# Scores of a Nyström attention: which matmul operand is read or written with a step

## The chip, the cores and the metric

The kernel runs on one core of one Trainium2 chip. Its metric is the time of one execution on the device, in microseconds.

## The reference, cut to what matters

Batch 4, 8 heads, 576 positions, 64 values per head; 32 landmarks, each the mean over 18 neighbouring positions. Three softmax matrices, a Newton iteration for a pseudo-inverse, and then two FFN layers (512 to 2048 to 512) over the 2304 tokens, one with mish, one with silu.

```python
q_lm = q.reshape(B, H, m, S // m, D).mean(axis=3)
k_lm = k.reshape(B, H, m, S // m, D).mean(axis=3)
...
A = sm(q, k_lm)
Bm = sm(q_lm, k_lm)
C = sm(q_lm, k)
Z = Bm.transpose(0, 1, 3, 2) / (...)
for _ in range(6):
    Z = 2 * Z - Z @ Bm @ Z
return (A @ Z @ C @ v).astype(np.float32)
...
x = _moe_ref(x=x, **moe_kwargs)
return _moe2_ref(x=x, **moe2_kwargs)
```

All of it is float32. The FFN's matmuls split each operand into a high and a low fp32r part and add three products (`PASSES`, L20).

## The kernel before, in words

**Attention.** The 32 pairs of batch and head are worked in eight groups of four heads (class `Group`, L1109). For a group, `load` (L1118) brings the keys `kn` and the queries `qn` as 128 partitions (4 heads x 32 landmarks) by 18 positions by 64 values, and `load_v` (L1135) the values. `transposed` (L1165) turns them into `Tk` and `Tq`, nine TensorE transposes each: the tile has 128 partitions (64 values of an even and of an odd position) and [9 position pairs, 4 heads, 32 landmarks] along a partition, so that neighbours along a partition are neighbouring landmarks, and two position pairs of one head lie 128 float32 apart. (Group 1 keeps its `Tk` and `Tq` in two borrowed tiles, which the trace calls `wp`.) `main` (L1203) makes the landmark means `lmT`, the small matrix Bm and the Newton steps.

`scores` (L1189) makes the scores of landmarks against positions: for four heads and two parities it issues eight matmuls of 64 x 32 weights out of `lmT` with 288 moving columns, on eight different 64*32 tiles of the array, into two PSUM banks (four heads in four times 32 partitions of each). TensorE runs each float32 matmul as two instructions, so a call is 16 of them in the trace. It is called twice for a group, by `c_side` (L1373) with the keys and by `a_side` (L1440) with the queries; the argument `mov` gives the moving operand of a head and parity. What comes next on the 288 columns: for C, VectorE's row maxima (`nm2`, L1385), ScalarE's exponentials `e_c` (L1395), and TensorE's transposes of 96 columns at a time; for A, VectorE's 32 x 32 transposes of the scores into `at` (L1453) and the softmax there.

The order of the columns in PSUM matters to these followers. The 288 columns of C are ordered as (w, l, c) and those of A as (l, j), in the letters of these two lines, in which c, w and j count position pairs and l landmarks:

```python
1, lambda e, h: kT[64 * e:64 * e + 64, :, h, :].rearrange("p (c w) l -> p w l c", c=VC)
s_, s_a = self.scores(0, lambda e, h: qT[64 * e:64 * e + 64, :, h, :].rearrange("p j l -> p l j"))
```

**FFN.** The first layer's units are matmuls on 128 x 128 tiles in fp32r (`emit_h`, L973, into `h`; `emit_o`, L1002, into `y`). They begin while the attention of later groups is still under way, and fill TensorE between its pieces. `projection` (L680) multiplies the first layer's weights `wa` by the attention's small matrices `ut`: 16 float32 TensorE instructions on the same eight 64*32 tiles, with 512 or 256 moving columns that are neighbours. Transposes of the identity (`y<-ident`, `h<-ident`, L1593) fill TensorE where nothing else is due.

**What sets the order.** All engines' programs are laid out when the kernel is built, by a planner (class `Line`, L70) with a cost for each instruction (`cost`, L101) and due times for chains of steps. The cost of a matmul goes by its number of columns and the size of its tile, not by steps in its operands. SyncE issues the loads in program order: group 2's `vn` takes the buffer of group 0's (two buffers, L1098 and L1136), and so waits for group 0's last C matmuls (`t<-vn,ect`, L1417); weights (`aw`, `wst`) are queued behind it.

Of the kernel before, what the change touches and what calls it, by code (L numbers as in the profile page):

```python
# [61 lines left out]
def f32(ap):  # L62
    return ap.bitcast(FP32)
# [347 lines left out]
def kernel(  # L411
# [15 lines left out]
    LM = 32  # L427
    J = S // LM
    J2 = J // 2
    SH = S // 2  # L430
# [4 lines left out]
    VC = 96 // LM  # L435
# [25 lines left out]
    def slots(n, of, **kw):  # L461
# [30 lines left out]
        out=twice.rearrange("p (a d) -> p a d", a=2),  # L492
# [18 lines left out]
    def until(cond):  # L511
        while not cond():
            yield "W"

    def marked(*m):
        return lambda: all(a in marks for a in m)
# [148 lines left out]
    def at_of(b):  # L665
        if b not in a_t:
            a_t[b] = at_p.tile([128, 2, GB, 2, SH], F32R, tag=f"at{b}", name=f"at{b}")
        return a_t[b]
# [434 lines left out]
    def bc(ap, n):  # L1103
        return ap.rearrange("p (j o) -> p j o", o=1).to_broadcast([128, ap.shape[1], n])
# [4 lines left out]
    class Group:  # L1109
# [76 lines left out]
            yield "W"  # L1186
            marks.add((g, "T" + nm))

        def scores(self, i, mov):  # L1189
            s = [self.pairs.take([128, 512], FP32) for e in range(2)]  # L1190
            for r in range(2):
                for h in range(HG):
                    e = (h + r) % 2
                    T.matmul(
                        out=s[e][0][32 * h:32 * h + 32, 0:SH],
                        lhsT=self.lmT[64 * e:64 * e + 64, i, 32 * h:32 * h + 32],
                        rhs=mov(e, h),
                        start=True,
                        stop=True,
                    )  # L1200
            return s, [x[0][:, 0:SH] for x in s]
# [171 lines left out]
        def c_side(self):  # L1373
            g = self.g
            yield from until(marked((g, "lmT"), (g, "Tk")))
            yield from until(lambda: self.pairs.open(2))
            kT = self.tT["k"]
            s_, s_c = self.scores(
                1, lambda e, h: kT[64 * e:64 * e + 64, :, h, :].rearrange("p (c w) l -> p w l c", c=VC)
            )  # L1380
            marks.add((g, "sc"))
            yield "V+"
            nm2 = s_p.tile([128, 2], FP32, tag="nm2", name="nm2")
            for e in range(2):
                V.tensor_reduce(out=nm2[:, e:e + 1], in_=s_c[e], axis=AX.X, op=ALU.max)  # L1385
            yield "V"
            nmc = s_p.tile([128, 1], FP32, tag="nmc", name="nmc")
            V.tensor_reduce(out=nmc, in_=nm2, axis=AX.X, op=ALU.max, negate=True)
            yield "A+"
            e_c = a_p.tile([128, 2, SH], FP32, tag="ec", name="ec", bufs=2)  # L1390
            scr = s_p.tile([128, 1], FP32, tag="scr", name="scr")
            scm = s_p.tile([128, 1], FP32, tag="scm", name="scm")
            sc2 = s_p.tile([128, 2], FP32, tag="sc2", name="sc2")
            for e in range(2):
                A.activation(out=e_c[:, e], in_=s_c[e], func=ACTF.Exp, bias=nmc, accum_out=sc2[:, e:e + 1])  # L1395
                Ring.give(s_[e])
            line.add(self.total(scm, sc2, scr), self.kind("N"), "V", line.end + 0.17)
            yield "T+"
            yield from until(lambda: g == 0 or (g - 1, "cv") in marks)
            ect = a_p.tile([96, VI, 128], FP32, tag="ect", name="ect")  # L1400
            for i0 in (0, 3):
                yield from until(self.banks.open)
                pe = self.banks.take([96, 3, 128], FP32)
                for i in range(i0, i0 + 3):
                    T.transpose(
                        out=pe[0][:, i - i0, :], in_=e_c[:, i % 2, 96 * (i // 2):96 * (i // 2) + 96], identity=ident
                    )
                yield "W"
                VA.copy(out=ect[:, i0:i0 + 3, :], in_=pe[0])
                Ring.give(pe)  # L1410
                yield "T+"
            yield from until(self.banks.open)
            pu_ = self.banks.take([128, D], FP32)
            pu = pu_[0]
            for i in range(VI):
                for h in range(HG):
                    T.matmul(  # L1417
                        out=pu[32 * h:32 * h + 32],
                        lhsT=ect[:, i, 32 * h:32 * h + 32],
                        rhs=self.vn[:, h, i, :],  # L1420
                        start=(i == 0),
                        stop=(i == VI - 1),
                    )
            marks.add((g, "cv"))
            yield "V"
            yield from until(lambda: (g, "y") in marks and ("w", scr.name) in line.seen)
            VAs.scaled(out=self.yu[:, LM:], in_=pu, scalar1=scr)
            Ring.give(pu_)
            yield "W"
            marks.add((g, "u"))  # L1430
# [9 lines left out]
        def a_side(self):  # L1440
            g = self.g
            yield from until(marked((g, "lmT"), (g, "Tq"), (g, "sc")))
            yield from until(lambda: self.pairs.open(2))
            qT = self.tT["q"]
            s_, s_a = self.scores(0, lambda e, h: qT[64 * e:64 * e + 64, :, h, :].rearrange("p j l -> p l j"))
            marks.add((g, "scores"))
            if g == 1:
                for t_ in self.borrowed:
                    Ring.give(t_)
            yield "V+"  # L1450
            at = a_p.tile([128, J, LM], FP32, tag="at", name="at", bufs=2)
            for e in range(2):
                V.transpose(out=at[:, e * J2:(e + 1) * J2, :].rearrange("p j l -> p (j l)"), in_=s_a[e])  # L1453
                Ring.give(s_[e])
            am = s_p.tile([128, J], FP32, tag="am", name="am")
            yield "V+"
            V.tensor_reduce(out=am, in_=at, axis=AX.X, op=ALU.max)
            yield "W"
            VP.tensor_tensor(out=at, in0=at, in1=bc(am, LM), op=ALU.subtract)
            yield "A+"  # L1460
            A.activation(out=at, in_=at, func=ACTF.Exp, scale=scale)
            yield "V+"
            asm = s_p.tile([128, J], FP32, tag="asm", name="asm")
            V.tensor_reduce(out=asm, in_=at, axis=AX.X, op=ALU.add)
            yield "V+"
            V.tensor_scalar(out=asm, in0=asm, scalar1=1e-9, scalar2=None, op0=ALU.add)
            ar = s_p.tile([128, J], FP32, tag="ar", name="ar")
            yield "V+"
            V.reciprocal(out=ar, in_=asm)
            yield "W"  # L1470
            VP.tensor_tensor(out=at, in0=at, in1=bc(ar, LM), op=ALU.mult)
            yield from until(lambda: g == 0 or (g - 1, "a_t") in marks)
            yield "V+"
            ar_t = a_p.tile([128, 2, SH], FP32, tag="a_t", name="a_t", bufs=1)
            V.transpose(out=ar_t.rearrange("p e n -> p (e n)"), in_=at.rearrange("p j l -> p (j l)"))
            yield "W"
            at = at_of(self.b)
            VA.copy(out=at[:, 0, self.hg], in_=ar_t)
            yield "W"
            (P if g < LOPOOL else VPx).tensor_tensor(out=at[:, 1, self.hg], in0=ar_t, in1=f32(at[:, 0, self.hg]), op=ALU.subtract)  # L1480
            a_ready[self.b, self.hg] = line.end + 0.12 + SLACK
            yield "W"
            marks.add((g, "a_t"))
# [53 lines left out]
    def o_time(u):  # L1537
        ph, t, f, first, last = u
        if first and not y_r.any_of(KD):
            return LATE  # L1540
        return max(g_ready.get((ph, t, f), LATE), w_ready.get(("o", 0, f), LATE))
# [3 lines left out]
    while todo or flight:  # L1545
# [32 lines left out]
        to = o_time(flight[0]) if flight else LATE  # L1578
# [81 lines left out]
```

## Time and profile before

| | us |
|---|---|
| median of 3 runs (832.25 to 833.1) | 832.32 |
| the profiled execution | 831.79 |
| its span in the trace | 830.0 |
| TensorE busy | 815.3 |
| VectorE busy | 561.9 |
| ScalarE busy | 443.2 |

The time of the profiled execution is 1.79 us longer than the span, in which the trace has its first and last record. A busy TensorE is one with a matmul under way, from its issue to its modelled end; matmuls overlap, so a batch is better measured from its first start to the start of what follows it. In the rows below, `64*32` after a matmul is the tile of the array, `64x288` what it reads, `t`, `y` and `h` are PSUM banks, and an idle time in brackets is that of the engine just before the row. All matmuls carry "f32" there; those of the FFN (`g,wo`, `wo,xg`, `at,wp`) are fp32r, those of the scores and the projections float32.

### The profile page before, as it was taken

How to read it: one execution, taken by the hardware profiler on the slowest of the kernel's cores; microseconds unless marked ns; L12 is line 12 of the kernel's file. 1: busy time of each engine (PE TensorE's matmuls, PEld its weight loads, DVE VectorE, ACT ScalarE, POOL GpSimd, SP SyncE). 2: the span in 40 equal slices, each digit the busy share in tenths (PEclk: the TensorE clock that was granted, in tenths of full speed). 3: DMA queues.
4: the chain of work that ended last, by engine and by line, in shares of the span. 5: the costliest groups of instructions: out<-in, count | busy, mean ns of one | idle time of the engine just before them, and what ended most of it. 6: DMA issues, size and time to landing. Idle time of an engine off the chain costs nothing.

```text
span 830.0 us, 15406 instructions
## 1 busy us (share of the span) xinstructions
PE 815.3 (98%) x5920; PEld 728.1 (88%) x5920; DVE 561.9 (68%) x1274; ACT 443.2 (53%) x981; POOL 124.7 (15%) x168
## 2 busy tenths in 40 slices
PE   9999999999999999999999999999999999999997
PEld 6787788777989999989998988988988988988985
DVE  7978876674667787853639999676655567555542
ACT  5475667757656656442526665436445436544422
POOL 2010321020000001000001122211232211232210
PEclk9999999999999999999999999999999999999999
DMA  8774024210044566541135222103100001100002
GB/s 279 237 212 160 29 87 127 67 39 30 29 143 154 169 199 199 174 147 46 60 101 174 77 102 92 36 1 106 48 1 0 1 1 37 40 0 1 1 1 76
DMA packets 41737, 72.29 MB, mean 87 GB/s; under 512 B 3776, under 2 KB 31936, under 8 KB 41664
## 3 DMA queue, kind: packets, MB, share of 16 engines
q1 hardware_dynamic: 40768, 70.53, 26.7%
q8 instruction: 46, 0.75, 0.4%
q10 hardware_dynamic: 896, 0.79, 0.3%
q14 instruction: 27, 0.22, 0.1%
HBM read 57.15 MB, written 14.16 MB: 86 GB/s over the span
## 4 chain that ended last, share of the span: by engine, by line
PE 93%; DVE 3%; DMA 2%; ACT 1%; issue 1%; ACTq 0%; SPq 0%
PE y L262 50%; PE h L262 34%; PE t L262 9%; DMA kn<-in_k_dram 1%; DMA wst<-in_moe_w_out_dram 1%; DVE m L262 0%; DVE wa L262 0%; DVE z L262 0%; ACT L262 0%; DMA out_dram<-z 0%; DVE lmk L262 0%; ACTq L274 0%; DVE nm L262 0%; DVE at L262 0%; DVE st L262 0%
## 5 line engine op out<-in xcount | busy, mean ns | idle before, releaser
L262 PE MATMUL y<-g,wo 128*128 128x288 f32 x1536 | 228.2, 300 | 0.6 <-DVE g L262 0.6
L262 PEld LDWEIGHTS y<-g,wo 128*128 128x128 f32 x1536 | 208.6, 188 | 16.8 <-issue 15.2
L262 PE MATMUL y<-wo,xg 128*128 128x512 f32 x693 | 180.0, 394 | 0.0
L262 PEld LDWEIGHTS y<-wo,xg 128*128 128x128 f32 x693 | 128.4, 188 | 20.8
L262 DVE TENSOR_TENSOR z<-h,z 128x384 f32<-128x384 f32 x161 | 87.7, 555 | 70.8 <-PE h L262 68.5
L262 PE MATMUL h<-at,wp 128*128 128x288 f32 x768 | 118.0, 300 | 0.7 <-ACT z L262 0.6
L262 PEld LDWEIGHTS h<-at,wp 128*128 128x128 f32 x768 | 105.3, 188 | 8.4 <-issue 6.5
L262 ACT ACTIVATE z<-h 128x288 f32<-128x288 f32 x128 | 51.5, 413 | 72.6 <-PE h L262 71.7
L262 DVE TENSOR_TENSOR g<-z,g 128x288 fp32r<-128x288 f32 x118 | 53.0, 461 | 51.0 <-ACT g L262 42.4
L262 ACT ACTIVATE z<-z 128x384 f32<-128x384 f32 x95 | 49.8, 525 | 34.4 <-DVE z L262 34.1
L262 PE MATMUL h<-xg,wp 128*128 128x384 f32 x288 | 57.8, 335 | 0.0
L262 PE MATMUL h<-xg,wf 128*128 128x384 f32 x282 | 56.6, 335 | 0.0
L262 DVE TENSOR_TENSOR xg<-z,xg 128x384 fp32r<-128x384 f32 x76 | 42.3, 557 | 20.2 <-ACT xg L262 20.1
L262 ACT CAST g<-z 128x288 fp32r<-128x288 f32 x120 | 49.9, 435 | 8.4 <-PE y L262 6.9
L262 PEld LDWEIGHTS h<-xg,wp 128*128 128x128 f32 x288 | 51.3, 188 | 3.2
L262 PEld LDWEIGHTS h<-xg,wf 128*128 128x128 f32 x282 | 50.3, 188 | 3.1
L262 DVE SCALAR_TENSOR_TENSOR m<-wst,m 128x512 int32<-128x512 int32 x64 | 46.4, 728 | 0.7
L262 PE MATMUL y<-wo,wp 128*128 128x512 f32 x171 | 44.9, 394 | 0.0
L262 ACT ACT_TABLE_LOAD x31 | 39.8, 1283 | 9.4 <-DVE nmc L262 3.5
L262 POOL TENSOR_TENSOR g<-z,g 128x288 fp32r<-128x288 f32 x10 | 8.4, 840 | 234.9 <-ACT g L262 156.5
L262 ACT CAST xg<-z 128x384 fp32r<-128x384 f32 x76 | 38.9, 512 | 1.6
L262 PEld LDWEIGHTS y<-wo,wp 128*128 128x128 f32 x171 | 31.7, 188 | 5.3
(245 smaller groups left out, 1164.8 us busy)
## 6 DMA issues: line engine op xcount, KB each, us to landing
wst<-in_moe_w_out_dram SPq DMA_DIRECT2D x32, 512.0 KB, 5.8
wst<-in_moe_w_in_dram SPq DMA_DIRECT2D x22, 512.0 KB, 5.2
kn<-in_k_dram SPq DMA_DIRECT2D x8, 576.0 KB, 6.2
vn<-in_v_dram SPq DMA_DIRECT2D x8, 576.0 KB, 6.6
yh<-ysb SPq DMA_DIRECT2D x32, 144.0 KB, 1.8
ysb<-yh SPq DMA_DIRECT2D x32, 144.0 KB, 3.0
ys<-ysb SPq DMA_DIRECT2D x32, 144.0 KB, 2.2
qn<-in_q_dram SPq DMA_DIRECT2D x7, 576.0 KB, 4.1
```

What stands on the lines that cost most here:

```text
L262: r = getattr(self.nc[e], name)(**kw)
```

## The change

`scores` takes a second function, `to`, which gives the order in which the 288 output columns are written. The moving operand keeps the order in which it lies in `Tk` and `Tq`: runs of 32 neighbouring landmarks, nine runs for a matmul. The output is written with a step instead, 3 columns for the keys and 9 for the queries, so that each score lands in the column where it was before. Number and order of the instructions are the same on each engine, and so are their waits; the forms of the 128 score matmuls differ.

```diff
-        def scores(self, i, mov):
+        def scores(self, i, mov, to):
...
-                        out=s[e][0][32 * h:32 * h + 32, 0:SH],
+                        out=to(s[e][0][32 * h:32 * h + 32, 0:SH]),
...
             s_, s_c = self.scores(
-                1, lambda e, h: kT[64 * e:64 * e + 64, :, h, :].rearrange("p (c w) l -> p w l c", c=VC)
+                1,
+                lambda e, h: kT[64 * e:64 * e + 64, :, h, :].rearrange("p (c w) l -> p c w l", c=VC),
+                lambda s: s.rearrange("p (w l c) -> p c w l", l=LM, c=VC),
             )
...
-            s_, s_a = self.scores(0, lambda e, h: qT[64 * e:64 * e + 64, :, h, :].rearrange("p j l -> p l j"))
+            s_, s_a = self.scores(
+                0, lambda e, h: qT[64 * e:64 * e + 64, :, h, :], lambda s: s.rearrange("p (l j) -> p j l", j=J2)
+            )
```

## Rows read from the trace of the kernel before

**Rows 1.** The page: TensorE's busy time, and the chain that ended last by engine.

```profile
PE 815.3 (98%) x5920; PEld 728.1 (88%) x5920; DVE 561.9 (68%) x1274; ACT 443.2 (53%) x981; POOL 124.7 (15%) x168
...
PE 93%; DVE 3%; DMA 2%; ACT 1%; issue 1%; ACTq 0%; SPq 0%
```

**Rows 2.** TensorE's waits, longest first: total us, times, longest us.

```profile
PE h L262 <- DVE z L262: 1.9, 1, 1.9
```

**Rows 3.** Score matmuls: duration ns min/median/max, first and last start us, forms.

```profile
L262 PE MATMUL t<-Tk,lmT x96: 492/500/511, 54.2 to 199.3; 64*32 64x288 f32 x96
L262 PE MATMUL t<-Tq,lmT x96: 727/766/786, 61.5 to 205.6; 64*32 64x288 f32 x96
```

**Rows 4.** TensorE's timeline, groups 2 and 3: start us, busy us, what.

```profile
54.21 1.05 PE L262 MATMUL t<-Tk,lmT 64*32 64x288 f32 x16
...
80.68 0.88 PE L262 MATMUL t<-Tk,lmT 64*32 64x288 f32 x16
81.49 2.17 PE L262 MATMUL h<-at,wp 128*128 128x288 f32 x14
...
93.39 1.40 PE L262 MATMUL t<-Tq,lmT 64*32 64x288 f32 x16
94.72 0.80 PE L262 MATMUL y<-g,wo 128*128 128x288 f32 x4
```

**Rows 5.** TensorE's timeline, two batches of projections and what follows each.

```profile
44.05 0.66 PE L262 MATMUL t<-wa,ut 64*32 64x256 f32 x16
44.64 1.59 PE L262 MATMUL h<-at,wp 128*128 128x288 f32 x10
...
121.11 1.09 PE L262 MATMUL t<-wa,ut 64*32 64x512 f32 x16
122.13 2.63 PE L262 MATMUL y<-g,wo 128*128 128x288 f32 x18
```

**Rows 6.** TensorE's groups by form: busy us, mean ns of one | idle before.

```profile
L262 PE MATMUL y<-g,wo 128*128 128x288 f32 x1536 | 228.2, 300 | 0.6 <-DVE g L262 0.6
L262 PE MATMUL y<-wo,xg 128*128 128x512 f32 x693 | 180.0, 394 | 0.0
...
L262 PE MATMUL t<-wa,ut 64*32 64x512 f32 x240 | 16.9, 601 | 0.0
...
L262 PE MATMUL t<-wa,ut 64*32 64x256 f32 x32 | 1.7, 388 | 0.1
```

**Rows 7.** VectorE's timeline, 54 to 98 us, where it waits for scores.

```profile
62.97 0.85 DVE L262 STREAM_TRANSPOSE at<-t 128x288 f32<-128x288 f32 x2 [0.95 <-PE t L262]
...
81.67 0.82 DVE L262 TENSOR_REDUCE nm<-t 128x1 f32<-128x288 f32 x2 [1.12 <-PE t L262]
```

**Rows 8.** TensorE's timeline, groups 0 and 1.

```profile
12.23 1.39 PE L262 MATMUL y<-Tq,lmT 64*32 64x288 f32 x16
...
15.41 2.07 PE L262 MATMUL y<-wp,lmT 64*32 64x288 f32 x29
17.41 0.53 PE L262 MATMUL t<-ident,ec 128*96 128x128 f32 x3
...
19.69 0.88 PE L262 MATMUL t<-vn,ect 96*32 96x64 f32 x48
```

**Rows 9.** VectorE's timeline, groups 0 and 1: its waits from 12 to 30 us.

```profile
12.56 0.82 DVE L262 TENSOR_REDUCE nm<-y 128x1 f32<-128x288 f32 x2 [0.53 <-PE y L262]
13.73 0.85 DVE L262 STREAM_TRANSPOSE at<-y 128x288 f32<-128x288 f32 x2 [0.35 <-PE y L262]
...
29.20 0.29 DVE L262 TENSOR_SCALAR wa<-wa 128x256 int32<-128x256 int32 x1 [0.68 <-ACT wa L262]
```

**Rows 10.** SyncE's timeline: the loads of group 2's values and of weights.

```profile
20.63 0.33 SPq L274 DMA_DIRECT2D vn<-in_v_dram  x1
21.01 3.37 SPq L274 DMA_DIRECT2D aw<-in_moe_w_in_dram  x4
```

**Rows 11.** ScalarE's timeline: its wait for the weights.

```profile
28.73 0.43 ACT L262 ACTIVATE wa<-aw 128x256 f32<-128x256 f32 x1 [3.48 <-DMA aw<-in_moe_w_in_dram]
```

## The prediction

> **What bounds the kernel now.** I read the page first. TensorE is busy for 98% of the span, and it makes up 93% of the chain that ended last [rows 1]: an edit on TensorE counts unless something else then holds the chain. The list of TensorE's waits says how often that happens: its longest wait in the whole run is 1.9 us, and it has that once [rows 2]. What lies behind the last scores (205.6 us [rows 3]) is a stream of matmuls whose inputs come out of earlier matmuls, so a microsecond won in the attention should stay won to the end.
>
> Then the instructions that the diff edits. Each group of four heads has two batches of score matmuls, "k" (for C) and "q" (for A), of 16 TensorE instructions each: eight matmuls, two instructions for each, on eight different tiles of the array. The reader is to see that k and q have the same shape, the same weights' shape and the same count, and yet one k instruction lasts 500 ns and one q instruction 766 ns [rows 3]. They differ in the order in which the moving operand is read: k takes 3 elements 1536 bytes apart and then goes one on, q takes 9 that are 512 bytes apart. So the order of reading sets the price. In the timeline a k batch occupies TensorE from its start to the start of the next instruction for 81.49 - 80.68 = 0.81 us, and a q batch for 94.72 - 93.39 = 1.33 us [rows 4]. The batches of the other groups look alike; only group 2's k batch is longer, with 1.05 us of busy time instead of 0.88 [rows 4].
>
> **What the change does to a batch.** It removes no instruction, adds none and moves none; no DMA, wait or queue is passed. In both batches the moving operand is now read in runs of 32 neighbours, and the output is written with a step: 3 columns for k, 9 for q. What VectorE and ScalarE read from PSUM afterwards lies where it lay, so their terms are nothing, without any cover.
>
> *The reading.* The trace has batches of the same kind that read neighbours: the projections, 16 instructions on eight 64*32 tiles. With 256 columns they occupy 44.64 - 44.05 = 0.59 us, with 512 columns 122.13 - 121.11 = 1.02 us [rows 5]. That is (1.02 - 0.59)/256 = 1.68 ns per column and 0.59 - 0.43 = 0.16 us fixed. For 288 columns: 0.16 + 0.48 = 0.64 us. So the k batch would win 0.81 - 0.64 = 0.17 us and the q batch 1.33 - 0.64 = 0.69 us, together 0.86 us per group, if writing costs nothing.
>
> *The writing.* No matmul before writes PSUM with a step, so its price is bounded. The lower end is nothing: the writes can't get cheaper than those of neighbouring columns in rows 5, which excludes a gain. The upper end is the worst price that the trace shows for a stepped access, the q reading: 1.33 us per batch, for both kinds. I take the lower end, for this reason. The fp32r matmuls of the FFN last 300 ns for 288 columns and 394 ns for 512, which is 0.42 ns per column, while the float32 matmuls of the projections last 388 ns for 256 and 601 ns for 512, which is 0.83 ns per column [rows 6]. PSUM thus takes columns twice as fast as one float32 instruction makes them, and the score matmuls are float32. A write that takes twice as long per column would still be covered, if the two steps which a float32 column takes end in one place one after the other. If they are instead two sweeps over all columns, this cover is gone, and that is the first rival.
>
> **Where the savings go.** The batches of groups 2 to 7 run from 54.2 to 205.6 us [rows 3], in the stage in which TensorE's order mixes attention and FFN. There the savings are 6 x 0.86 = 5.2 us. VectorE is the engine that could be late next. But it waits for the scores: 0.95 us ahead of group 2's q transposes, 1.12 us ahead of group 3's k maxima [rows 7]. By the latter point groups 2 and 3 have saved 0.17 + 0.69 + 0.17 = 1.03 us, so VectorE's gap just holds it. I count the 5.2 us in full.
>
> Groups 0 and 1 lie in the first 20 us: the q batch at 12.23 us and both batches of group 1 from 15.41 to 17.41 us [rows 8]. That is 1.7 us of TensorE work. In this stage VectorE and the loads count too. VectorE waits 0.53 us for group 0's k scores and 0.35 us for its q scores, and then has no idle time until 28.5 us [rows 9]. On the other side, group 2's values are loaded into a buffer that group 0's last C matmuls (from 19.69 us) free, and SyncE issues that load at 20.63 us, with the first layer's weights queued behind it at 21.01 us [rows 8, 10]. ScalarE later waits 3.48 us for these weights, and VectorE 0.68 us for ScalarE [rows 9, 11]. So an earlier TensorE also brings the weights earlier. Between 0 and 1.7 us I take 0.8 us, near the middle, because VectorE's own two waits let it start its run at most 0.9 us earlier.
>
> **Sum**: 5.2 + 0.8 = 6.0 us off. The profiled execution took 831.79 us, which gives 825.8 us. The median of the three runs shown, 832.32 us, is 0.5 us above it, so the forecast for a median is **826.3 us**. Its own range is 825.4 us (all 6.9 us are kept) to 828.8 us (the first two groups give nothing, and a third of the rest is taken up by VectorE).
>
> **The rivals.**
>
> *1. PSUM takes stepped columns at half the rate, and float32 doesn't cover it.* Then the 0.48 us of columns in a batch become 0.97 us and a batch 1.13 us. k loses 0.32 us, q wins 0.20 us: 0.12 us lost per group, 1.0 us in all, 833.3 us, which I call no change: 0.2%, or 1.7 us, is about what a measurement of this kernel can tell from nothing. For it: the write of neighbours is known only at two columns per 0.83 ns, and nothing in the trace shows the two steps of a float32 column side by side. Against it: the cover of rows 6.
> This rule stands in the Trainium skill, Advanced Engine Details and Errata, section Memory Cachelines: PSUM is accessed in lines of two float32 values, and any pattern that isn't contiguous slows matmuls considerably. No run here shows it yet; by it the change would come out near this rival's time. The same section asks for at least two hits on a 16-byte line of SBUF. The trace agrees only in part: both k and q leave the line after each element, and q pays far more than k [rows 3].
>
> *2. The stepped write is as dear as the stepped read of q (the other side: slower).* Both batches then take 1.33 us. q wins nothing and k loses 0.52 us, 8 x 0.52 = 4.2 us, 836.5 us. It decides from a price per column that I can give: k and q now take 0.81 + 1.33 = 2.14 us together, so they break even at 1.07 us each, which is (1.07 - 0.16)/288 = 3.2 ns per column, 1.9 times the price of neighbours. From 2.1 times on the loss is over 0.2%; below 1.7 times the gain is over 0.2%. For it: a stepped access on the other side of the same instruction does cost 2.4 times (1.33 - 0.16 = 1.17 us against 0.48 us). Against it: k reads with a step as well, and pays 0.65 us, 1.35 times; so step alone isn't dear.
>
> *3. The savings are taken up.* VectorE or the weights hold the chain in the attention, and only about half is left: 3 us, 829.3 us. For it: VectorE's gaps of about 1 us are hardly larger than what is saved ahead of them [rows 7]. Against it: TensorE hardly waits for VectorE [rows 1, 2].
>
> *4. The change doesn't do what it says*: q's 766 ns come from something other than the order of reading, and both batches stay as they are, 832.3 us. Little speaks for it, since k and q share everything else [rows 3].
>
> **How the numbers follow.** The forecast has 0.52, rival 3 has 0.08: faster 0.60. Rival 1 has 0.15 and rival 4 has 0.03: same 0.18. Rival 2, with prices from 2.1 times upward, has 0.22. The range reaches from 824.8 us, a little below the forecast's own low end, to 834.5 us: it takes in the forecast, rivals 1, 3 and 4, and the mild end of rival 2, and leaves out 836.5 us.
>
> **What the profile after would show.** Right: k and q instructions of equal length, about 388 + 32 x 0.83 = 415 ns; batches of 0.64 us both in groups 3 to 7; VectorE's waits for at and nm shorter; the attention's last group some 6 us earlier, and the rest unchanged. The reading is right but the writing isn't free: equal k and q instructions, longer than 415 ns; at about 415 + 240 = 655 ns rival 1 holds, at 766 ns rival 2. If k and q still differ, the write's price depends on its step, 3 against 9 columns. If the batches shrink as forecast and the time doesn't, rival 3 holds, and TensorE's waits for VectorE or the loads will have grown. The forecast is wrong as soon as one batch takes more than about 0.97 us, the point where the gain falls below 0.2%.

## The result, and the profile after

| | before | after |
|---|---|---|
| median, us | 832.71 (6 runs, 832.25 to 834.81) | 825.88 (6 runs, 825.0 to 828.75) |
| ratio to before | 1 | 0.9917, 95% interval 0.9896 to 0.9938 |
| profiled execution / its span, us | 831.79 / 830.0 | 827.49 / 825.7 |
| TensorE busy, us | 815.3 | 808.5 |

The changed kernel is faster by 6.8 us, 0.8%. The forecast was 826.3 us, which is 6.0 us less than the 832.3 us it started from.

First the score matmuls, in the view of one tile's instructions (duration ns min/median/max, first and last start us, forms), to be held against [rows 3]:

```profile
L262 PE MATMUL t<-Tk,lmT x96: 402/415/427, 54.5 to 195.1; 64*32 64x288 f32 x96
L262 PE MATMUL t<-Tq,lmT x96: 402/415/428, 61.6 to 201.0; 64*32 64x288 f32 x96
```

Both kinds last 415 ns, where they were 500 and 766 ns. The last one starts at 201.0 instead of 205.6 us. The batches in TensorE's timeline, against [rows 4]:

```profile
80.02 0.71 PE L262 MATMUL t<-Tk,lmT 64*32 64x288 f32 x16
80.66 2.36 PE L262 MATMUL h<-at,wp 128*128 128x288 f32 x14
...
92.57 0.72 PE L262 MATMUL t<-Tq,lmT 64*32 64x288 f32 x16
93.22 0.79 PE L262 MATMUL y<-g,wo 128*128 128x288 f32 x4
```

A k batch takes 80.66 - 80.02 = 0.64 us and a q batch 93.22 - 92.57 = 0.65 us. Held against before, group 3's k batch starts 0.66 us earlier than in [rows 4], what follows it 0.83 us, its q batch 0.82 us, and what follows that 1.50 us: the gain comes at the batches. VectorE's waits for scores, against [rows 7]:

```profile
62.39 0.85 DVE L262 STREAM_TRANSPOSE at<-t 128x288 f32<-128x288 f32 x2 [0.36 <-PE t L262]
...
80.84 0.82 DVE L262 TENSOR_REDUCE nm<-t 128x1 f32<-128x288 f32 x2 [0.95 <-PE t L262]
```

VectorE still waits, 0.36 us where it was 0.95, and 0.95 us where it was 1.12.

One part of the profiled execution has nothing to do with the change: the first loads came later. TensorE's timeline of the kernel after has two waits for them which the profiled execution of before hadn't:

```profile
8.20 0.55 PE L262 MATMUL h<-ident,kn 128*128 128x128 f32 x3 [1.41 <-DMA kn<-in_k_dram]
...
10.39 0.52 PE L262 MATMUL h<-ident,wp 128*128 128x128 f32 x3 [0.44 <-DMA wp<-in_q_dram]
...
12.78 0.24 PE L262 MATMUL t<-lmT 64*32 64x32 f32 x5
```

The same row in the kernel before, where group 0's scores could begin:

```profile
11.50 0.24 PE L262 MATMUL t<-lmT 64*32 64x32 f32 x5
```

So this execution began its scores 1.28 us later, and yet ended 4.3 us earlier. It is also the second slowest of the six. The experiments' profiles, with edits that can't touch the loads, have these matmuls anywhere between 11.7 and 12.7 us. Part of the spread of a few microseconds among runs comes in here, and two profiles are only compared from this point on.

### The profile page after: what moved, and what is told of

It reads as the page before. It is cut to its first block, busy times and chain, and to the rows that moved or that the text cites. A ratio compares the mean times of both kernels' runs of the same rounds, so it can differ in the third digit from the quotient of the medians.

```text
span 825.7 us, 15406 instructions
## 1 busy us (share of the span) xinstructions
PE 808.5 (98%) x5920; PEld 727.3 (88%) x5920; DVE 562.3 (68%) x1274; ACT 443.1 (54%) x981; POOL 124.6 (15%) x168
## 4 chain that ended last, share of the span: by engine, by line
PE 92%; DVE 4%; DMA 1%; ACT 1%; issue 1%; ACTq 0%; SPq 0%
PE y L262 50%; PE h L262 34%; PE t L262 8%; DMA wp<-in_q_dram 1%; DVE m L262 1%; DVE wa L262 0%; DVE at L262 0%; DVE z L262 0%; DMA out_dram<-z 0%; DVE lmk L262 0%; ACTq L274 0%; DVE g L262 0%; DVE wp L262 0%; DVE nm L262 0%; ACT wp L262 0%
```

## The experiments

**The theory.** The order in which the moving operand is read sets the length of a score instruction; the stepped write costs a second step per column, which float32 covers; and what TensorE saves goes through to the end. Rivals: something of the queries themselves made them slow; a stepped write costs nothing in any case; part of the saving is taken up by VectorE or the loads.

### One kind of scores alone

Keys only (e1), the queries' line as it was before:

```diff
-                0, lambda e, h: qT[64 * e:64 * e + 64, :, h, :], lambda s: s.rearrange("p (l j) -> p j l", j=J2)
+                0, lambda e, h: qT[64 * e:64 * e + 64, :, h, :].rearrange("p j l -> p l j"), lambda s: s
```

Expected: 

> Only the keys' scores read neighbours and write with a step of 3; the queries' scores are as before. If the two batches add up along TensorE's stream: k instructions 415 ns, q instructions 766 ns, k batches 0.64 us, and 8 x 0.17 = 1.4 us off the time before. If a stage takes part of it up (the rival), under 0.7 us off.

Queries only (e2), the keys' lines as they were before:

```diff
-                lambda e, h: kT[64 * e:64 * e + 64, :, h, :].rearrange("p (c w) l -> p c w l", c=VC),
-                lambda s: s.rearrange("p (w l c) -> p c w l", l=LM, c=VC),
+                lambda e, h: kT[64 * e:64 * e + 64, :, h, :].rearrange("p (c w) l -> p w l c", c=VC),
+                lambda s: s,
```

Expected: 

> Only the queries' scores read neighbours and write with a step of 9; the keys' scores are as before. If the two batches add up: k instructions 500 ns, q instructions 415 ns, and 8 x 0.68 = 5.4 us off the time before, the rest of the change's 6.8 us. If the gains overlap or are taken up, e1 and e2 together differ from the change by more than 1.5 us.

| | median, us | ratio to before (832.75 us) |
|---|---|---|
| e1, keys only | 832.3 | 0.9991 (0.9980 to 1.0002) |
| e2, queries only | 827.89 | 0.9939 (0.9923 to 0.9954) |

The instructions have the expected lengths, here of e1 and then of e2:

```profile
L262 PE MATMUL t<-Tk,lmT x96: 402/415/427, 54.8 to 198.8; 64*32 64x288 f32 x96
L262 PE MATMUL t<-Tq,lmT x96: 692/762/786, 61.9 to 205.0; 64*32 64x288 f32 x96
```

```profile
L262 PE MATMUL t<-Tk,lmT x96: 492/500/508, 53.6 to 195.3; 64*32 64x288 f32 x96
L262 PE MATMUL t<-Tq,lmT x96: 402/415/427, 60.9 to 201.2; 64*32 64x288 f32 x96
```

The queries bring 0.61% or 5.1 us. By its times the keys' share, 0.09%, can't be told from nothing, nor from the expected 1.4 us, since its interval reaches from a gain of 1.7 us to a loss of 0.2 us. Together they make 5.8 us against the change's 6.8 us, less than 1.5 us apart, so the two add up as far as the times can tell. The traces tell more, at the end of the next part.

### Where in the program the savings lie

Both edits under a condition on the group, `g < 2` in e3 and `g > 1` in e4; the other groups are as before:

```diff
...
+                (lambda e, h: qT[64 * e:64 * e + 64, :, h, :]) if g < 2
+                else lambda e, h: qT[64 * e:64 * e + 64, :, h, :].rearrange("p j l -> p l j"),
+                (lambda s: s.rearrange("p (l j) -> p j l", j=J2)) if g < 2 else lambda s: s,
...
```

Expected of e3: 

> The change in groups 0 and 1 alone, the first 20 us. The prediction's sum has 0.8 us off for them. If all of TensorE's work counts there, 1.7 us off; if the loads and VectorE hold this stage, 0 to 0.3 us off.

Expected of e4: 

> The change in groups 2 to 7 alone. The prediction's sum has 5.2 us off for them, counted in full. If VectorE takes part of it up, under 4 us off.

| | median, us | ratio to before (832.75 us) |
|---|---|---|
| e3, groups 0 and 1 | 831.6 | 0.9983 (0.9971 to 0.9994) |
| e4, groups 2 to 7 | 828.39 | 0.9945 (0.9930 to 0.9960) |

Groups 2 to 7 bring 4.6 us by the ratio, with an interval from 3.3 to 5.8 that holds the 5.2 us counted for them, and also the rival's under 4 us. Groups 0 and 1 bring 1.4 us, with an interval from 0.5 to 2.4 that holds both the 0.8 and the 1.7 us and excludes that the loads take it up wholly. The two profiles say more here, because in both of them the first loads came alike: the matmuls in front of group 0's scores start at 12.73 us in each. The timelines of TensorE and of SyncE in e3, where groups 0 and 1 are changed:

```profile
12.73 0.24 PE L262 MATMUL t<-lmT 64*32 64x32 f32 x5
...
19.51 0.88 PE L262 MATMUL t<-vn,ect 96*32 96x64 f32 x48
...
51.38 0.27 PE L262 MATMUL t<-lmT 64*32 64x32 f32 x8
```

```profile
20.45 0.33 SPq L274 DMA_DIRECT2D vn<-in_v_dram  x1
```

And in e4, where they are not:

```profile
12.73 0.25 PE L262 MATMUL t<-lmT 64*32 64x32 f32 x5
...
20.91 0.88 PE L262 MATMUL t<-vn,ect 96*32 96x64 f32 x48
...
52.80 0.27 PE L262 MATMUL t<-lmT 64*32 64x32 f32 x8
```

```profile
21.85 0.33 SPq L274 DMA_DIRECT2D vn<-in_v_dram  x1
```

The C matmuls that free group 0's values start 1.40 us earlier, the load of group 2's values and the weights behind it go out 1.40 us earlier, and 30 us later group 2's landmark matmuls still start 1.42 us earlier. So the loads move with TensorE. ScalarE's wait for these weights ends 1.67 us earlier, first e3 and then e4:

```profile
28.42 0.45 ACT L262 ACTIVATE wa<-aw 128x256 f32<-128x256 f32 x1 [2.81 <-DMA aw<-in_moe_w_in_dram]
```

```profile
30.09 0.43 ACT L262 ACTIVATE wa<-aw 128x256 f32<-128x256 f32 x1 [3.63 <-DMA aw<-in_moe_w_in_dram]
```

The same can be done for the whole attention: a profile's stretch from group 0's landmark matmuls (12.73 us above, 11.50 us before, 12.78 us after) to group 2's, and from these to what follows the last q batch. It leaves out the first loads and all that comes after the attention. What follows the last q batch starts at 206.12 us in e3 and at 202.50 us in e4. The marks before, after, in e1 and in e2 (in these two group 0's matmuls start at 12.59 and 12.06 us):

```profile
51.46 0.27 PE L262 MATMUL t<-lmT 64*32 64x32 f32 x8
...
206.26 1.06 PE L262 MATMUL h<-at,wp 128*128 128x288 f32 x6
```

```profile
51.70 0.27 PE L262 MATMUL t<-lmT 64*32 64x32 f32 x8
...
201.34 1.06 PE L262 MATMUL h<-at,wp 128*128 128x288 f32 x6
```

```profile
52.01 0.27 PE L262 MATMUL t<-lmT 64*32 64x32 f32 x8
...
205.67 1.06 PE L262 MATMUL h<-at,wp 128*128 128x288 f32 x6
```

```profile
50.82 0.27 PE L262 MATMUL t<-lmT 64*32 64x32 f32 x8
...
201.54 1.06 PE L262 MATMUL h<-at,wp 128*128 128x288 f32 x6
```

| | groups 0 and 1, us | groups 2 to 7, us |
|---|---|---|
| before | 39.96 | 154.80 |
| e3, groups 0 and 1 changed | 38.65 | 154.74 |
| e4, groups 2 to 7 changed | 40.07 | 149.70 |
| after | 38.92 | 149.64 |
| e1, keys only | 39.42 | 153.66 |
| e2, queries only | 38.76 | 150.72 |

The stretch of groups 2 to 7 repeats to 0.06 us where the scores are alike. There the change saves 5.16 us (before to after) and 5.04 us (e3 to e4), so the 5.2 us counted are kept in full. The keys alone save 1.14 us and the queries alone 4.08 us, together 5.22 us: the keys' share is real, and the two add up. The stretch of groups 0 and 1 repeats less well: the change saves 1.04 us there from before to after, and 1.42 us from e4 to e3, where TensorE has 1.7 us less work.

### What the stepped write costs

e5 takes the step out of the write:

```diff
-                lambda s: s.rearrange("p (w l c) -> p c w l", l=LM, c=VC),
+                lambda s: s.rearrange("p (j l) -> p j l", l=LM),
...
-                0, lambda e, h: qT[64 * e:64 * e + 64, :, h, :], lambda s: s.rearrange("p (l j) -> p j l", j=J2)
+                0, lambda e, h: qT[64 * e:64 * e + 64, :, h, :], lambda s: s.rearrange("p (j l) -> p j l", l=LM)
```

Expected: 

> The scores read neighbours and also write neighbours, so the score columns lie in another order and what follows takes them as they lie: the softmaxes mix up positions, at the same sizes and durations. If the step in the write is free: instructions of 415 ns and batches of 0.64 us, and the time of the change, 826 us. If the step costs something that the change still pays, shorter instructions, and 0.1 us per batch of it would show as 1.6 us less time.

Measured: 826.55 us, ratio 0.9917 (0.9897 to 0.9936), the same ratio as that of the change, and instructions of the same length:

```profile
L262 PE MATMUL t<-Tk,lmT x96: 402/415/427, 53.2 to 193.9; 64*32 64x288 f32 x96
L262 PE MATMUL t<-Tq,lmT x96: 402/415/427, 60.3 to 199.7; 64*32 64x288 f32 x96
```

For these float32 matmuls the step in the write is free. Whether it is free in itself or covered by float32, as the prediction argued, is told apart by instructions with one step per column. Two kernels put eight bf16 matmuls of a tile of ones ahead of each batch of scores, into the same columns; in the second of them the output has a step of 9, cut here to its matmul:

```diff
...
+                    nc.tensor.matmul(
+                        out=x.rearrange("p (l j) -> p j l", j=J2),
+                        lhsT=ones[64 * e:64 * e + 64, 0:32],
+                        rhs=ones[64 * e:64 * e + 64].rearrange("p (j l) -> p j l", j=J2),
+                        start=True,
+                        stop=True,
+                    )
...
```

Expected without the step: 

> The changed kernel with eight more matmuls ahead of each batch of scores, on the same tiles and into the same PSUM columns, of ones in bf16 (one instruction each, one step per column), 288 columns, written as neighbours; the scores then overwrite them. It is the measure for the next run: one instruction of one step per column should last 176 + 288 x 0.42 = about 296 ns.

Expected with the step: 

> As the run before, but the bf16 ones are written with a step of 9 columns. If PSUM takes stepped columns at half the rate and float32's two steps per column covered it: about 416 ns, 120 ns more than neighbours. If a stepped write costs nothing at all and there was nothing to cover: as the neighbours, about 296 ns.

Measured, first the neighbours and then the step of 9 (view of the tile `ones`):

```profile
L1197 PE MATMUL t<-ones x96: 279/293/294, 53.1 to 200.4; 64*32 64x288 bf16 x96
```

```profile
L1197 PE MATMUL t<-ones x96: 399/413/414, 53.7 to 202.3; 64*32 64x288 bf16 x96
```

The step adds 120 ns, and 120/288 is 0.42 ns per column, as much again as the 0.42 ns of a column written to its neighbour [rows 6]: a stepped column takes twice the time. In the timeline a bf16 batch and the scores behind it take 79.56 - 78.83 = 0.73 us with neighbours and 80.54 - 79.69 = 0.85 us with the step, 0.12 us more. (The two kernels ran once each, 827.23 and 828.68 us; the changed kernel's six runs spread over more than that.)

```profile
78.83 0.32 PE L1197 MATMUL t<-ones 64*32 64x288 bf16 x8
78.96 0.67 PE L262 MATMUL t<-Tk,lmT 64*32 64x288 f32 x16
79.56 2.27 PE L262 MATMUL h<-at,wp 128*128 128x288 f32 x14
```

```profile
79.69 0.43 PE L1197 MATMUL t<-ones 64*32 64x288 bf16 x8
79.90 0.71 PE L262 MATMUL t<-Tk,lmT 64*32 64x288 f32 x16
80.54 2.15 PE L262 MATMUL h<-at,wp 128*128 128x288 f32 x14
```

So there is a price in bf16, and none in float32. That float32's second step per column hides it is an inference, but the sizes fit: 0.83 ns for a stepped column, and 0.83 ns in which a float32 instruction makes one. The last kernel on this writes the first layer's fp32r matmuls, which also take one step per column, in pairs of neighbours:

```diff
-            T.matmul(out=h[0][:, :n], lhsT=w, rhs=x, start=(i == 0), stop=(i == len(ops) - 1))
+            T.matmul(out=h[0][:, :n].rearrange("p (a b t) -> p b a t", t=2, b=9), lhsT=w, rhs=x.rearrange("p (b a t) -> p b a t", t=2, b=9), start=(i == 0), stop=(i == len(ops) - 1))
```

Expected: 

> The changed kernel with the first layer's 768 fp32r matmuls into h (288 columns, 128x128) written in pairs of neighbouring columns, with pairs 18 columns apart; mish takes h's columns in that order, so tokens are mixed up. If a step costs only where it splits a pair: 300 ns as before and the time of the change, 826 us. If any step costs as much as a second step per column: 420 ns, and up to 768 x 0.12 = 92 us more.

Measured: 826.18 us in one run, and the view of groups by form has them at 300 ns as in the kernel after:

```profile
L262 PE MATMUL h<-at,wp 128*128 128x288 f32 x768 | 118.2, 300 | 0.6 <-ACT z L262 0.5
```

Pairs of neighbours cost nothing here, where each column takes one step. No run writes fp32r singly or bf16 in pairs, so it isn't shown that it is the pair which makes this write free, and not the fp32r matmul on its larger tile. The result agrees with the Trainium skill, Advanced Engine Details and Errata, section Memory Cachelines, that PSUM goes by lines of two float32 values; the same section's sentence that any pattern that isn't contiguous slows matmuls significantly holds for bf16 written singly (413 against 293 ns), and not for float32 (415 ns either way) nor for pairs.

### What the stepped read costs

e7 exchanges the two old reading orders between keys and queries:

```diff
-                lambda e, h: kT[64 * e:64 * e + 64, :, h, :].rearrange("p (c w) l -> p c w l", c=VC),
+                lambda e, h: kT[64 * e:64 * e + 64, :, h, :].rearrange("p j l -> p l j"),
...
-                0, lambda e, h: qT[64 * e:64 * e + 64, :, h, :], lambda s: s.rearrange("p (l j) -> p j l", j=J2)
+                0, lambda e, h: qT[64 * e:64 * e + 64, :, h, :].rearrange("p (c w) l -> p w l c", c=VC), lambda s: s
```

Expected: 

> Neighbours are written; the keys are read in the queries' order of before (9 positions 512 bytes apart, then one on) and the queries in the keys' order of before (3 positions 1536 bytes apart). The columns' order is wrong for what follows. If the order of reading sets the price: 766 ns for the keys, 500 ns for the queries, and 832 us. If something of the queries themselves made them slow: as before, 500 and 766 ns.

```profile
L262 PE MATMUL t<-Tk,lmT x96: 649/762/784, 54.6 to 199.9; 64*32 64x288 f32 x96
L262 PE MATMUL t<-Tq,lmT x96: 492/500/512, 62.4 to 206.3; 64*32 64x288 f32 x96
```

The lengths have changed places, and the time of the one run is 831.54 us: the order sets the price. e9 asks what of the order it is, with three near places for the keys and pairs of neighbours for the queries:

```diff
...
+                lambda e, h: kT[64 * e:64 * e + 64, :, h, :].rearrange("p (w c) l -> p w l c", c=VC),
+                lambda s: s,
...
+                lambda e, h: qT[64 * e:64 * e + 64, :, h, :].rearrange("p j (l t) -> p l j t", t=2),
+                lambda s: s.rearrange("p (l j t) -> p l j t", j=J2, t=2),
```

Expected: 

> Neighbours are written; the keys are read 3 positions at a time that are only 512 bytes apart, then one on; the queries are read in pairs of neighbours, 9 pairs 512 bytes apart. The columns' order is wrong for what follows. If the number of places visited in turn sets the price, and not how far they lie apart: 500 ns for the keys; if the distance of 512 bytes does: near 766 ns. For the queries: if the price is per place visited, a pair shares it and the extra 350 ns falls to 175 ns or less, so under 590 ns; if two hits on a place cover it wholly, 415 ns.

```profile
L262 PE MATMUL t<-Tk,lmT x96: 492/500/509, 53.8 to 195.9; 64*32 64x288 f32 x96
L262 PE MATMUL t<-Tq,lmT x96: 402/437/474, 61.0 to 201.9; 64*32 64x288 f32 x96
```

Three places 512 bytes apart cost what three places 1536 bytes apart do, 500 ns. So it isn't the distance that made the queries dear, but the nine places in turn. Two neighbours at each of nine places bring 766 ns down to 437 ns, nearly to the 415 ns of runs. The time of the one run was 828.06 us.

The last kernel, e8, keeps the old steps in the read and adds steps in the write:

```diff
...
+                lambda e, h: kT[64 * e:64 * e + 64, :, h, :].rearrange("p (c w) l -> p w l c", c=VC),
+                lambda s: s.rearrange("p (c w l) -> p w l c", c=VC, l=LM),
...
+                lambda e, h: qT[64 * e:64 * e + 64, :, h, :].rearrange("p j l -> p l j"),
+                lambda s: s.rearrange("p (j l) -> p l j", l=LM),
```

Expected: 

> The scores read with the steps of the kernel before and write with a step too (positions 32 or 96 columns apart), so every access on either side leaves its neighbour; what follows takes the columns in a wrong order. If the write is free and the read alone sets the price: 500 ns for the keys and 766 ns for the queries, as before, and 832 us. If a stepped write costs but was covered up to now by a spare half of the time per column, the same; if it adds, more than 550 and 820 ns.

```profile
L262 PE MATMUL t<-Tk,lmT x96: 492/500/511, 55.3 to 200.4; 64*32 64x288 f32 x96
L262 PE MATMUL t<-Tq,lmT x96: 727/766/786, 62.6 to 206.7; 64*32 64x288 f32 x96
```

500 and 766 ns, and 832.36 us in one run: for these float32 matmuls a stepped write adds nothing to a stepped read.

## Why the prediction was right, point by point

**The price of reading** held to the hundredth: batches of 0.64 us were forecast from the projections [rows 5], and 0.64 and 0.65 us were measured in group 3. Instructions of 415 ns were forecast, and 415 ns measured. That the order of reading is the cause was argued from two kinds of batch that share everything else; e7 has shown it.

**The price of writing** was the open term, taken at its lower end because float32 puts out a column in 0.83 ns and PSUM takes one in 0.42 ns [rows 6]. e5 shows that the change pays nothing, and the bf16 pair bears out the reason: a stepped column costs double there, 0.83 ns, which is just what float32 takes for a column anyway. So rival 1 was right on the rate and wrong on the missing cover, and rival 2 is out by the 415 ns, where it asked for 766 ns.

**Groups 2 to 7** were counted in full at 5.2 us; e4 measured 4.6 us with an interval that holds it, and the traces have 5.0 to 5.2 us up to the end of the attention. The text held that VectorE's gap of 1.12 us would be nearly used up by 1.03 us saved ahead of it. That step was wrong, though it did no harm: the gap shrank by 0.17 us alone, group 3's own k batch, since VectorE had itself been waiting for group 2's q scores and moved forward with TensorE (its wait there went from 0.95 to 0.36 us). A gap is used up by what is saved since the last point at which the engine waited, not by the whole sum.

**Groups 0 and 1** were taken at 0.8 us, near the middle between nothing and 1.7 us. That term was a little small: e3 measured 1.4 us with an interval that holds 0.8 us too, the profiles of e3 and e4 show 1.42 us, and those of before and after 1.04 us. The step that failed is that VectorE's two small waits limit the gain to 0.9 us. They do so for a while: until 28 us most of VectorE's rows start 0.85 to 0.90 us earlier in e3 than in e4. But what TensorE saved brought the load of group 2's values, and the weights in the queue behind it, forward by 1.40 us, and VectorE's wait for ScalarE and these weights further on [rows 9], 0.82 us in e4, is gone in e3 and let it follow:

```profile
28.90 0.29 DVE L262 TENSOR_SCALAR wa<-wa 128x256 int32<-128x256 int32 x1
```

```profile
30.56 0.29 DVE L262 TENSOR_SCALAR wa<-wa 128x256 int32<-128x256 int32 x1 [0.82 <-ACT wa L262]
```

The prediction named this path [rows 8 to 11], but gave it only half a weight.

**The sum**: 6.0 us forecast; e3 and e4 together make 1.4 + 4.6 = 6.0 us, and the change itself measured 6.8 us, with an interval from 5.2 to 8.7 us. The remaining 0.8 us between the parts and the whole is within the spread of the runs, and nothing more is made of it. That 826.3 us lies only 0.4 us from the measured 825.88 us owes something to luck: the median before rose from 832.32 to 832.71 us with three more runs, and from there the same sum gives 826.7 us.

**Rival 3** is out for the attention, where 6.20 of the 6.9 us of TensorE's work are kept between the marks of before and after. That a microsecond won there stays won to the end holds less strictly: the profiled executions differ by 5.6 us from group 0's marks to the end. Two waits behind the attention took the 0.6 us, first before and then after:

```profile
249.37 1.05 PE L262 MATMUL h<-at,wp 128*128 128x288 f32 x6 [0.55 <-ACT z L262]
...
454.56 1.33 PE L262 MATMUL h<-x,wp 128*128 128x384 f32 x6 [1.85 <-DVE z L262]
```

```profile
244.81 1.06 PE L262 MATMUL h<-at,wp 128*128 128x288 f32 x6 [0.91 <-ACT z L262]
...
450.22 1.33 PE L262 MATMUL h<-x,wp 128*128 128x384 f32 x6 [2.08 <-DVE z L262]
```

Just ahead of the first of them ScalarE had itself waited for weights (`wst`), 0.67 us before and 1.03 us after, and the wait varies whatever the edit: 0.18 us in e4, 1.42 us in e1, none listed in e7 and e8. So it is a part of the spread of the times, and not shown to be a price of the change. **Rival 4** is out by the durations.

## What to carry to other kernels

Where one side of a matmul has to be stepped, step the write and read the moving operand in runs, as long as the matmul is float32: a stepped write of single columns was free there (415 ns either way) and cost bf16 120 ns on top of 293. A batch with neighbouring operands on the same tiles, elsewhere in the same trace, priced this edit to the hundredth of a microsecond. On an engine that makes up nearly the whole chain, small savings added up batch by batch, and a load that was queued behind this engine's work moved with it. Where a saving is smaller than the spread of the times, a stretch of the trace between two marks, chosen to leave out what varies, can still show it: 1.14 us for the keys, where the times of e1 show nothing.

## What was not expected

In these matmuls the cost of a stepped read goes by how many places are visited in turn, not by how far they lie apart: three places cost 85 ns on top of 415, at 512 as at 1536 bytes, and nine cost 350 ns. Two neighbours at each place take away nearly all of it (22 ns are left). No run here tried numbers between three and nine, so where the step lies isn't known.
